# Fewer weight conversions in the first steps of attention, the 1e-9 added on GpSimd, and the scaled decay stored from another tile

## The chip, the cores and the metric

One core of a Trainium2 chip runs the whole program. The metric is the device time of one execution in microseconds (us), the median of three. The engines are TensorE (PE, its weight loads are PEld), VectorE (DVE), ScalarE (ACT), GpSimd (POOL) and SyncE (SP), whose queue issues nearly all DMA transfers. Each engine takes its instructions in the order in which they stand in the program, so an instruction that waits holds everything behind it on its engine.

## The reference

```python
# q, k, v: [4, 8, 576, 64], f: [4, 8, 576]
scores = scale * np.matmul(q, k.transpose(0, 1, 3, 2))
log_f = np.log(np.clip(f, 0.0001, 1.0))
cum = np.cumsum(log_f, axis=-1)
decay = cum[:, :, :, None] - cum[:, :, None, :]
scores = np.where(causal, -1000000000.0, scores + decay)
scores = scores - np.max(scores, axis=-1, keepdims=True)
attn = np.exp(scores)
attn = attn / (np.sum(attn, axis=-1, keepdims=True) + 1e-09)
x = np.matmul(attn, v)                    # then laid out as [2304, 512]
...
gate = 1.0 / (1.0 + np.exp(-(x @ w_gate)))     # w_gate, w_val: [512, 1536]
x = gate * (x @ w_val) @ w_out                 # w_out: [1536, 512]
...
h = x @ w_in                                   # [512, 2048]
out = (h * np.clip(h + 3.0, 0.0, 6.0) / 6.0) @ w_out2
```

## The kernel before

The weights arrive as float64 and are converted to pairs of float32 (a rounded part and the rest); the dense layers multiply such pairs with three matmuls each (`mm3`).

**Attention in steps.** The 16 pairs of heads are cut into four blocks of queries each; a block is a unit, and step t of the main loop (t = 0 to 66) starts unit t, so that pair p holds steps 4p to 4p + 3. Pairs 0 to 6 take their blocks upwards, the last block being the short one (64 queries of both heads together); pairs from 7 on (`KT`) take them downwards, load their queries and keys in another layout and transpose them on DVE. For a unit, PE computes scores into the banks `st` (`scores`); DVE adds the decay `dc` (`dt` for the short block, in which POOL has masked the future, `tail_decay`) and takes the least value in one pass (`least`, L500), into a tile `e` of the pool `ep`, which has seven buffers; ACT takes the exponential in place and sums it (L508); `norm` adds 1e-9 to the sums, takes the reciprocal on DVE (L543, L544) and has POOL scale `e` (L546). Step t runs `norm` for unit t - 1 and `flip` for unit t - 3: PE transposes `e` into `tt`, ACT copies that to `etA` and `etB`. At the last block of a pair, `values` multiplies with v, and `store` writes the result to DRAM, from where the first dense layer loads it again.

**Other work in the steps.** From step 4 on `conv.run` pays a rate into an account at each step; whenever it holds 1.0, one half (512 columns of 128 rows) of a weight tile is converted. A half is L107 and L108 on DVE, L111 on ACT, L114 on DVE, then the rounded part and the rest: both on POOL up to step 15 (L64, L65), on ACT (L62) and POOL (L65) from step 16. The halves come in the order `wg`, `wg`, `wv`, `wv`, `wg`, `wg`, `wv`, `wv`, four of `wo`, and four that are used only after attention. From step 23 on `fill.one()` puts one group of the first dense layer (12 matmuls of 512 columns: `pg`, `pv` or `po`) in each step, from step 30 on without those that hold `values`. A group whose weights' conversion has not been issued yet is not placed; the step then has no group, and all groups left are placed after attention.

**The scaled decay.** Pairs from 7 on need the decay times -8. `cumulate` makes the cumulative sum `cum` from the logarithms `fl`; after step 2 DVE writes the scaled copy to `eight`, a tile of the pool `ep`, and a DMA stores it in `cum_d[1]` (L1369, L1370). `fl` comes from the pool `ax` (two buffers, tag `x`), whose next use is the output tile `x` of `values`.

Of the kernel before, what the change touches and what calls it, by code (L numbers as in the profile page):

```python
# [7 lines left out]
F32 = mybir.dt.float32  # L8
# [4 lines left out]
ALU = mybir.AluOpType  # L13
# [7 lines left out]
def attn_moe_kernel(  # L21
# [13 lines left out]
    nc = tc.nc  # L35
    B, H, S, D = q.shape
# [3 lines left out]
    P = 128  # L40
    NP = H // 2
    NKT = 5
    NQ = 4
# [150 lines left out]
    conv = Converter()  # L194
# [43 lines left out]
    ep = att.enter_context(tc.tile_pool(name="ep", bufs=7))  # L238
# [50 lines left out]
    def cumulate():  # L289

        fl, one = (ax.tile([P, 2, S], F32, tag="x", name=nm)[: B * H] for nm in ("fl", "ones"))
        fl, ones, pick = fl[:, 0], one[:, 0], one[:, 1, : 2 * P].rearrange("p (j c) -> p j c", j=2)
        cum = ep.tile([P, S], F32, tag="e", name="cum")[: B * H]
        nc.scalar.dma_start(fl, f.rearrange("b h s -> (b h) s"))
        nc.vector.memset(ones, 1.0)
        nc.vector.tensor_scalar(fl, fl, 1.0e-4, 1.0, ALU.max, ALU.min)
        nc.scalar.activation(fl, fl, AF.Ln)
        nc.scalar.activation(one[:, 1, 2 * P : 2 * P + 1], fl[:, :1], AF.Exp)
        for j in range(2):
            nc.vector.tensor_scalar(pick[:, j], ones[:, :P], ident[: B * H, j : j + 1], 1.0, ALU.mult, ALU.mult)  # L300
        nc.vector.tensor_tensor_scan(cum, ones, fl, 0.0, ALU.mult, ALU.add)
        nc.sync.dma_start(cum_d[0], cum)
        return cum, pick

    def behind(i):
        return tc.issue_after(i.ins) if i is not None else ExitStack()
# [14 lines left out]
    class Pair:  # L321
# [217 lines left out]

        def norm(self, s):  # L540
            m, n = self.m[s], len(self.es[s])
            with behind(reads[-1]), tc.high_priority():
                nc.vector.tensor_scalar(m[:, 8 : 8 + n], m[:, 4 : 4 + n], 1.0e-9, None, ALU.add)  # L543
                pace["dve"] = nc.vector.reciprocal(m[:, 12 : 12 + n], m[:, 8 : 8 + n])  # L544
            for j, e in enumerate(self.es[s]):
                pace["pool"] = nc.gpsimd.tensor_scalar(e, e, m[:, 12 + j : 13 + j], 1.0, ALU.mult, ALU.mult)  # L546
# [504 lines left out]
    class Second:  # L1051
# [93 lines left out]
        def unit(self, k, x, ys, temps, between={}):  # L1145
            u1, u2, p5 = temps
            g, tt = self.ga[k % 2], nc.vector.tensor_tensor
            r11, r22, r12 = self.act(u1, g, 0, 0), self.act(p5, g, 1, 1), self.act(u2, g, 1, 0)
            r21 = self.act(x(), g, 0, 1)
            then = {1: (r11,), 2: (r11,), 3: (r11,), 4: (r22,), 5: (r12, r22, r22), 6: (r21, r12, r12, r21, r21)}  # L1150
            for s in range(7):
                if s in (1, 3):
                    y = ys.pop(0)()
                o = y if s % 2 else x()
                self.product(o, k, s, s in (0, 1, 3))
                if s in (0, 2, 3):
                    nc.scalar.copy({0: u1, 2: u2, 3: p5}[s], o)  # L1157
                elif s < 6:
                    c = {1: u1, 4: p5, 5: u2}[s]
                    tt(c, c, o, ALU.add)  # L1160
                for r in then.get(s, ()):
                    next(r)
                if k % NQ2 == NQ2 - 1:
                    self.load_block(k // NQ2 * 7 + 7 + s)
                if s in between:
                    between[s]()
# [59 lines left out]
    def warm_up(n):  # L1226
        if not warm:
            warm["z"] = a1.tile([P, 256], F32, tag="z", name="z").bitcast(BF16)
            with tc.high_priority():
                nc.vector.memset(warm["z"], 0.0)  # L1230
        z = warm["z"]
        for _ in range(n):
            o = psF.tile([P, 512], F32, tag="F", name="o")
            pe.matmul(o, z[:, :P], z, start=True, stop=True)
# [4 lines left out]
    EA = (nc.scalar, nc.gpsimd, nc.gpsimd)  # L1239
    EF = (nc.scalar, nc.scalar, nc.gpsimd)  # L1240
    WU = (8, 4, 4, 4)

    KD, KT, RT = 4, 7, 0

    CA, C0, CB, CC = 0.65, 4, (1.8, 1.0, 1.5, 1.7, 2.0), 1.0

    CE, CS = 0.38, 0.12


    NGA, NCA, GA = 2, 3, 1  # L1250

    NSA = 8
# [16 lines left out]
    units = [(p, s) for p in pairs for s in p.order]  # L1269
    pe.rows = True  # L1270
    warm_up(WU[0])
    cum, pick = cumulate()
    pairs[0].load()
    pairs[1].load()
    pairs[0].load_v()
# [88 lines left out]
    for t in range(len(units) + 3):  # L1364
        for job in (fixed, expo, norm, prep):
            job(t)
        if t == 2:
            eight = ep.tile([P, S], F32, tag="e", name="eight")[: B * H]
            nc.vector.tensor_scalar(eight, cum, -8.0, 1.0, ALU.mult, ALU.mult)  # L1369
            nc.sync.dma_start(cum_d[1], eight)  # L1370
        p, s = unit(t - 4)
        if p and s == p.order[-1] and p.hp == NP - 1 and p.b < NCA:
            done = p.b + 1
        p, s = unit(t - 5)
        if p and s == p.order[-1] and t < len(units) + 3:
            fill.load(p.b, p.hp + 1)
        if t >= C0:
            conv.run(CS if len(conv.jobs) <= 2 * NSA - 6 * NGA else CE if t < NQ * (KT - 1) else CA, EA if t < NQ * KD else EF)
        fill.n = done
    att.close()  # L1380
    pace["dve"] = None
# [63 lines left out]
```

## Time and profile before

| what | value |
|---|---|
| time, median of 3 (lowest, highest) | 1002.28 us (1002.18, 1002.36) |
| profiled execution, its own time | 1003.57 us |
| its span, first to last instruction | 1001.8 us |
| PE busy | 986.5 us (98%), 5733 matmuls |
| DVE, ACT, POOL busy | 530.9, 476.9, 290.5 us |
| mean granted TensorE clock | 0.998 |

Busy time is the union of an engine's instructions; a matmul's end is modelled, so a busy PE is not PE at its peak. The span leaves 1.77 us of the profiled execution outside, and the profiled execution is 1.29 us above the median.

### The profile page before, as it was taken

To read this page: it belongs to the slowest core of one execution; us is meant where nothing else is said; L and a number is where in the kernel's file an instruction comes from. 1 tells how busy PE (TensorE), PEld (TensorE's weight loads), DVE (VectorE), ACT (ScalarE), POOL (GpSimd) and SP (SyncE) were. 2 spreads that over 40 slices of the span, in tenths; PEclk is the share of its full clock that TensorE was granted. 3 is DMA by queue.
4 is the path that set the end of the run, shared out by engine and by line. 5 is a ranking of instruction groups with operands and counts; after the bars stand their busy time and mean duration, and the time that the engine had idled before them with its cause. 6 is when DMAs were issued, how large, how long until landed. Compare 5 with 4: busy or idle time off the path is not lost.

```text
span 1001.8 us, 16150 instructions
## 1 busy us (share of the span) xinstructions
PE 986.5 (98%) x5733; PEld 810.4 (81%) x5733; DVE 530.9 (53%) x1220; ACT 476.9 (48%) x1094; POOL 290.5 (29%) x360
## 2 busy tenths in 40 slices
PE   8889999999999999999999999999999999999998
PEld 4556766667688889988888888899899898998987
DVE  6777856645347543737777574553534443333322
ACT  6787677667634432424434343453444443433322
POOL 3675655545323220302334131111111111111110
PEclk9999999999999999999999999999999999999999
DMA  7999796744324352566977578654686845753211
GB/s 184 294 250 226 198 244 156 185 143 145 119 79 154 117 166 82 175 210 264 331 258 252 179 270 318 245 198 166 237 330 206 293 147 193 294 209 148 81 66 64
DMA packets 141072, 197.30 MB, mean 197 GB/s; under 512 B 84192, under 2 KB 93408, under 8 KB 136896
## 3 DMA queue, kind: packets, MB, share of 16 engines
q1 hardware_dynamic: 140944, 196.20, 59.9%
q8 instruction: 45, 0.74, 0.3%
q14 instruction: 35, 0.29, 0.1%
q10 hardware_dynamic: 48, 0.07, 0.0%
HBM read 142.88 MB, written 53.36 MB: 196 GB/s over the span
## 4 chain that ended last, share of the span: by engine, by line
PE 91%; DVE 3%; ACT 2%; DMA 2%; issue 1%; POOL 0%; SPq 0%; DVEq 0%; ACTq 0%; POOLq 0%
PE po L216 34%; PE pv L216 18%; PE u L216 17%; PE pg L216 15%; PE st L216 4%; PE tt L220 3%; DVE e L500 1%; DMA kn<-in_k_dram 1%; ACT e L508 1%; DMA cum_d<-eight 1%; DMA x_d<-x 0%; DVE raw L108 0%; ACT raw L111 0%; ACT etB L580 0%; PE o L216 0%
## 5 line engine op out<-in xcount | busy, mean ns | idle before, releaser
L216 PE MATMUL po<-w,big 128*128 128x512 f32 x864 | 200.5, 390 | 0.0
L216 PEld LDWEIGHTS po<-w,big 128*128 128x128 f32 x864 | 161.8, 188 | 32.8
L216 PE MATMUL pg<-big,wg 128*128 128x512 f32 (+1 forms) x720 | 161.9, 371 | 0.0
L216 PE MATMUL pv<-big,wv 128*128 128x512 f32 (+1 forms) x720 | 161.4, 371 | 0.0
L216 PE MATMUL po<-big,wo 128*128 128x512 f32 (+1 forms) x720 | 160.9, 371 | 0.2 <-DVE big L65 0.2
L216 PEld LDWEIGHTS pg<-big,wg 128*128 128x128 f32 x720 | 125.8, 189 | 27.2 <-issue 4.0
L216 PEld LDWEIGHTS pv<-big,wv 128*128 128x128 f32 x720 | 125.6, 189 | 26.8 <-issue 4.5
L216 PEld LDWEIGHTS po<-big,wo 128*128 128x128 f32 x720 | 125.6, 189 | 25.7 <-issue 2.2
L1160 DVE TENSOR_TENSOR h<-h,u 128x384 f32<-128x384 f32 x69 | 38.2, 554 | 154.0 <-PE u L216 154.0
L546 POOL TENSOR_SCALAR e<-e,m 128x256 f32<-128x256 f32 (+4 forms) x144 | 86.8, 617 | 48.8 <-DVE m L544 32.1
L508 ACT ACTIVATE e<-e,m 128x256 f32<-128x256 f32 (+4 forms) x144 | 83.6, 584 | 31.6 <-DVE m L500 20.3
L216 PE MATMUL u<-h,big 128*128 128x384 f32 x504 | 90.2, 336 | 0.4 <-DVE h L1160 0.4
L216 PE MATMUL u<-h,h 128*128 128x384 f32 x504 | 90.1, 336 | 0.0
L216 PEld LDWEIGHTS u<-h,big 128*128 128x128 f32 x504 | 88.3, 188 | 1.8 <-DVE h L1160 0.8
L216 PEld LDWEIGHTS u<-h,h 128*128 128x128 f32 x504 | 88.4, 188 | 1.0
L1109 POOL TENSOR_TENSOR big<-tail,big 128x384 fp32r<-128x384 f32 x30 | 30.5, 1018 | 196.5 <-PE u L216 115.5
L1157 ACT COPY h<-u 128x384 f32<-128x384 f32 x69 | 32.8, 475 | 111.5 <-PE u L216 111.5
L500 DVE CUSTOM_DVE_ANT_0 e<-st,dc 128x384 f32<-128x384 f32 (+3 forms) x110 | 53.5, 520 | 47.9 <-PE st L216 30.3
L872 DVE SCALAR_TENSOR_TENSOR sg<-sg,pv 128x512 f32<-128x512 f32 (+1 forms) x48 | 29.7, 618 | 92.3 <-PE pv L216 59.7
L111 ACT ACTIVATE raw<-raw 128x512 f32<-128x512 f32 x68 | 45.6, 682 | 67.1 <-DVE raw L108 64.5
L62 ACT CAST big<-sg 128x512 fp32r<-128x512 f32 (+1 forms) x60 | 34.8, 580 | 60.6 <-DVE sg L872 54.6
L114 DVE SCALAR_TENSOR_TENSOR raw<-raw 128x512 int32<-128x512 int32 x68 | 52.5, 782 | 19.4 <-ACT raw L111 18.9
(141 smaller groups left out, 1202.8 us busy)
## 6 DMA issues: line engine op xcount, KB each, us to landing
h<-xc_d SPq DMA_DIRECT2D x21, 768.0 KB, 7.2
big<-x_d SPq DMA_DIRECT2D x28, 512.0 KB, 5.8
raw<-in_moe_w_out_dram SPq DMA_DIRECT2D x28, 512.0 KB, 3.7
h<-wt_d SPq DMA_DIRECT2D x12, 1024.0 KB, 7.4
big<-wt_d SPq DMA_DIRECT2D x12, 1024.0 KB, 7.6
x_d<-x SPq DMA_DIRECT2D x16, 576.0 KB, 3.9
h<-wb_d SPq DMA_DIRECT2D x12, 768.0 KB, 4.6
big<-wb_d SPq DMA_DIRECT2D x12, 768.0 KB, 5.2
```

Of the source, the lines that this page charges most:

```text
L62: nc.scalar.copy(hi, src)
L111: nc.scalar.activation(e, e, AF.Copy, scale=2.0**-112)
L114: nc.vector.scalar_tensor_tensor(low, high, 3, low, ALU.logical_shift_left, ALU.bitwise_or)
L216: i = nc.tensor.matmul(*a, **k)
L220: i = nc.tensor.transpose(*a)
L500: i = nc.vector.tensor_tensor_reduce(out=e, in0=st, in1=d, op0=ALU.add, op1=ALU.min, scale=self.by, scalar=init, accum_out=m[:, a : a + 1],)
L508: nc.scalar.activation(e, e, AF.Exp, bias=m[:, a : a + 1], scale=-1.0, accum_out=m[:, 4 + b : 5 + b])
L546: pace["pool"] = nc.gpsimd.tensor_scalar(e, e, m[:, 12 + j : 13 + j], 1.0, ALU.mult, ALU.mult)
L872: pace["dve"] = nc.vector.scalar_tensor_tensor(sg, sg, 1.0, pv, ALU.add, ALU.mult)
L1109: (nc.vector if f else nc.gpsimd).tensor_tensor(lo, sg, hi.bitcast(F32), ALU.subtract)
L1157: nc.scalar.copy({0: u1, 2: u2, 3: p5}[s], o)
L1160: tt(c, c, o, ALU.add)
```

## The change

The account's rate is 0.24 instead of 0.38 in the first stretch, and that stretch ends at step 20 instead of 23; the rate of 0.65 behind it is the same. The 1e-9 is added on POOL, ahead of POOL's scaling of the same unit, and DVE's reciprocal waits for it. The scaled decay is written into `fl` instead of a tile of `ep`.

```diff
-        return cum, pick
+        return cum, pick, fl
...
     def norm(self, s):
         m, n = self.m[s], len(self.es[s])
+        with tc.high_priority():
+            nc.gpsimd.tensor_scalar(m[:, 8 : 8 + n], m[:, 4 : 4 + n], 1.0e-9, 1.0, ALU.add, ALU.mult)
         with behind(reads[-1]), tc.high_priority():
-            nc.vector.tensor_scalar(m[:, 8 : 8 + n], m[:, 4 : 4 + n], 1.0e-9, None, ALU.add)
             pace["dve"] = nc.vector.reciprocal(m[:, 12 : 12 + n], m[:, 8 : 8 + n])
...
-    CE, CS = 0.38, 0.12
+    CE, CS, CT = 0.24, 0.12, 21
...
-    cum, pick = cumulate()
+    cum, pick, eight = cumulate()
...
         if t == 2:
-            eight = ep.tile([P, S], F32, tag="e", name="eight")[: B * H]
             nc.vector.tensor_scalar(eight, cum, -8.0, 1.0, ALU.mult, ALU.mult)
             nc.sync.dma_start(cum_d[1], eight)
...
-            conv.run(CS if len(conv.jobs) <= 2 * NSA - 6 * NGA else CE if t < NQ * (KT - 1) else CA, EA if t < NQ * KD else EF)
+            conv.run(CS if len(conv.jobs) <= 2 * NSA - 6 * NGA else CE if t < CT else CA, EA if t < NQ * KD else EF)
```

On DVE, at the turn from step 6 to step 7 (the two L500 of 512 columns are unit 6, the one from `dt` is unit 7, L646 makes `x` for the finished pair), the kernel before has:

```order
L500 ISA e,m<-st,dc 128x512
L500 ISA m 128x1
L543 TENSOR_SCALAR m<-m 128x2
L544 RECIPROCAL m<-m 128x2
L107 TENSOR_SCALAR raw<-raw 128x512
L646 TENSOR_TENSOR x<-pv,x 128x256
L108 SCALAR_TENSOR_TENSOR raw<-raw 128x512
L114 SCALAR_TENSOR_TENSOR raw<-raw 128x512
L646 TENSOR_TENSOR x<-pv,x 128x320
L500 ISA e,m<-st,dt 128x288
```

The changed kernel has there (one line number higher):

```order
L500 ISA e,m<-st,dc 128x512
L500 ISA m 128x1
L545 RECIPROCAL m<-m 128x2
L647 TENSOR_TENSOR x<-pv,x 128x256
L647 TENSOR_TENSOR x<-pv,x 128x320
L500 ISA e,m<-st,dt 128x288
```

The first half's three DVE instructions have gone to step 8, and the add to POOL. On PE, at steps 32 to 35 (the first row is the transpose for unit 29, the next the scores of unit 32), the kernel before has:

```order
L220 MATMUL tt<-ident,e 128x64 x16
L216 MATMUL st<-kp,qz_144 128x288 x2
L216 MATMUL po<-big,wo_1692 128x512 x6
L216 MATMUL po<-big,wo_1883 128x512 x6
L220 MATMUL tt<-ident,e 128x64 x12
L216 MATMUL st<-kp,qp 128x512 x2
L216 MATMUL po<-big,wo_1692 128x512 x6
L216 MATMUL po<-big,wo_1883 128x512 x6
L220 MATMUL tt<-ident,e 128x64 x12
L216 MATMUL st<-kp,qp 128x384 x2
L216 MATMUL pv<-etB,vn_152 64x320 x6
```

The changed kernel has there:

```order
L220 MATMUL tt<-ident,e 128x64 x16
L216 MATMUL st<-kp,qz_144 128x288 x2
L220 MATMUL tt<-ident,e 128x64 x12
L216 MATMUL st<-kp,qp 128x512 x2
L220 MATMUL tt<-ident,e 128x64 x12
L216 MATMUL st<-kp,qp 128x384 x2
L216 MATMUL pv<-etB,vn_152 64x320 x6
```

Steps 32 and 33 hold no group any more; all later groups move by two places, and two stand behind attention that stood in it. On POOL, from unit 6's scaling to unit 8's (the 512-column L547 is unit 6, the 576-column one unit 7), the changed kernel has:

```order
L543 TENSOR_SCALAR m<-m 128x2
L547 TENSOR_SCALAR e<-e,m 128x512 x2
L386 AFFINE_SELECT dt<-dc 64x576 x2
L543 TENSOR_SCALAR m<-m 128x1
L547 TENSOR_SCALAR e<-e,m 128x576
L543 TENSOR_SCALAR m<-m 128x4
L547 TENSOR_SCALAR e<-e,m 128x128
```

Before, POOL had the same rows without the L543; now unit 7's add stands behind two masking passes for the next pair.

## Rows read from the trace of the kernel before

**Rows 1.** Stretch, length; busy PE, PEld, DVE, ACT, POOL; granted clock; DMA share, GB/s.

```profile
25.00:83.00 58.00, 50.21 (x500) 30.65 (x498) 45.40 (x163) 47.99 (x148) 41.78 (x60) 0.97 0.99 264
83.00:136.00 53.00, 52.13 (x380) 35.78 (x380) 39.30 (x118) 37.25 (x99) 31.10 (x41) 1.00 0.83 214
136.00:980.00 844.00, 843.56 (x4629) 716.96 (x4626) 423.78 (x865) 370.25 (x791) 206.13 (x233) 1.00 0.57 195
```

**Rows 2.** Timeline of DVE, steps 6 and 7: start, duration, [idle before <- releaser].

```profile
27.46 0.69 DVE L500 CUSTOM_DVE_ANT_0 e<-st,dc 128x512 f32<-128x512 f32 x1 [1.30 <-DMA cum_d<-eight]
...
28.36 0.41 DVE L107 TENSOR_SCALAR raw<-raw 128x512 int32<-128x512 int32 x1
...
31.50 0.45 DVE L500 CUSTOM_DVE_ANT_0 e<-st,dt 128x288 f32<-128x288 f32 x1
...
32.55 0.79 DVE L543 TENSOR_SCALAR m<-m 128x2 f32<-128x2 f32 x1
```

**Rows 3.** Timeline of PE, the scores of units 7 and 8.

```profile
28.61 1.24 PE L216 MATMUL st<-kp,qz 128*128 128x288 f32 x4
...
32.02 0.51 PE L216 MATMUL st<-masks,identb 128*128 128x384 bf16 x2 [2.06 <-DVE m L500]
```

**Rows 4.** Busy time by microsecond, one row of the stretch behind that wait.

```profile
33.00:34.00 1.00, 1.00 (x14) 1.00 (x12) 0.85 (x4) 1.00 (x4) 0.31 (x1) 0.50 1.20 191
```

**Rows 5.** Timeline of DVE, least values at steps 3, 11, 15, 19 and 23.

```profile
18.17 0.46 DVE L500 CUSTOM_DVE_ANT_0 e<-st,dt 128x288 f32<-128x288 f32 x1 [0.37 <-PE st L216]
...
43.94 0.46 DVE L500 CUSTOM_DVE_ANT_0 e<-st,dt 128x288 f32<-128x288 f32 x1 [0.31 <-PE st L216]
...
57.68 0.45 DVE L500 CUSTOM_DVE_ANT_0 e<-st,dt 128x288 f32<-128x288 f32 x1
...
69.73 0.45 DVE L500 CUSTOM_DVE_ANT_0 e<-st,dt 128x288 f32<-128x288 f32 x1
...
83.20 0.45 DVE L500 CUSTOM_DVE_ANT_0 e<-st,dt 128x288 f32<-128x288 f32 x1
```

**Rows 6.** One line's instructions, 20 to 136 us: ns least/median/most, first and last start.

```profile
L108 DVE SCALAR_TENSOR_TENSOR raw<-raw x12: 741/866/1123, 29.0 to 121.4; 128x512 int32<-128x512 int32 x12
...
L111 ACT ACTIVATE raw<-raw x12: 667/680/743, 29.8 to 122.3; 128x512 f32<-128x512 f32 x12
...
L114 DVE SCALAR_TENSOR_TENSOR raw<-raw x12: 683/694/993, 30.5 to 123.0; 128x512 int32<-128x512 int32 x12
```

**Rows 7.** Timelines of POOL and DVE: a half's rest; unit 15's masking and reciprocal.

```profile
32.02 1.30 POOL L65 TENSOR_TENSOR wg<-raw,wg 128x512 fp32r<-128x512 f32 x1
...
61.58 1.40 POOL L386 TENSOR_SCALAR_AFFINE_SELECT dt<-dc 64x576 f32<-64x576 f32 x2
...
61.87 0.15 DVE L544 RECIPROCAL m<-m 128x1 f32<-128x1 f32 x1
```

**Rows 8.** Groups of 25 to 83 us: busy us, mean ns | idle before.

```profile
L546 POOL TENSOR_SCALAR e<-e,m 128x128 f32<-128x128 f32 x10 | 3.7, 373 | 3.3 <-ACT e L508 1.3 <-DVE m L544 1.2 <-PE tt L220 0.7
L543 DVE TENSOR_SCALAR m<-m 128x2 f32<-128x2 f32 x9 | 3.0, 335 | 0.0
```

**Rows 9.** Timeline of PE, steps 32 to 34.

```profile
125.17 1.24 PE L216 MATMUL st<-kp,qz 128*128 128x288 f32 x4
126.03 2.80 PE L216 MATMUL po<-big,wo 128*128 128x512 f32 x10
...
131.17 3.06 PE L216 MATMUL po<-big,wo 128*128 128x512 f32 x12
...
135.37 1.03 PE L216 MATMUL pv<-etB,vn 128*64 128x320 f32 x6
```

**Rows 10.** Timeline of DVE, the least values of units 32 and 33.

```profile
127.55 0.45 DVE L500 CUSTOM_DVE_ANT_0 e<-st,dt 128x288 f32<-128x288 f32 x1
...
131.37 0.69 DVE L500 CUSTOM_DVE_ANT_0 e<-st,dc 128x512 f32<-128x512 f32 x1 [1.23 <-POOL e L546]
```

**Rows 11.** Timeline of SP's queue, the store of the scaled decay.

```profile
21.49 0.51 SPq L1370 DMA_DIRECT2D cum_d<-eight  x1
```

## Prediction

> **What bounds the kernel now.** I read the busy time by stretch first. From 136 to 980 us PE is busy 843.56 of 844 us: nothing there waits, and no edit here changes PE's work, so time can be won or lost only ahead of it. From 25 to 83 us, the steps before the first group of the dense layer, PE is busy 50.21 of 58 us, with a mean granted clock of 0.97, while ACT is busy 48 and DVE 45; from 83 to 136 us it is busy 52.13 of 53 [rows 1]. So 7.8 us of idle PE and, by the clock (0.03 of 58), up to 1.7 us of slow PE lie in the first stretch, and 0.9 us in the second. The timelines of DVE and PE then show one place in detail: unit 6's least value waits 1.30 us for the DMA from `eight`, whose buffer it takes over; behind it stand the first half's instructions, L107 at 28.36, and unit 7's least value comes only at 31.50 [rows 2], 2.9 us after its scores began at 28.61; PE, which needs that bank, waits 2.06 us [rows 3]. Behind this wait the granted clock is 0.50, the lower of its two levels, 1.2 GHz [rows 4].
>
> **When the halves come.** The account gives the steps. Before: 0.38 from step 4 passes whole numbers at steps 6, 9, 11, 14, 17, 19 and 22, then with 0.65 at 24, 26, 27, 29 and 30. After: 0.24 passes at 8, 12, 16 and 20, then 0.65 at 22, 23, 25, 27, 28, 30, 31 and 33. Up to step 22 there are five halves in place of seven. The last `wo` half is issued at step 33 in place of 30, so steps 32 and 33 have no `po` to place, as the order on PE shows.
>
> **The first stretch: gain.** Take as a measure the least value of the short block, once in four steps. It starts at 18.17, 31.50, 43.94, 57.68, 69.73 and 83.20 [rows 2, 5]; the pitches are 13.3, 12.4, 13.7, 12.1 and 13.5 us, with 1, 1, 2, 1 and 2 halves. After they hold 0, 1, 1, 1 and 2.
> - Steps 3 to 7: both the wait for `eight` and the half go. Unit 7's scores start at 28.61 because PE still multiplies with v until then, so DVE can begin on its first bank half-way through these scores (1.24 us, [rows 3]), at about 29.3 in place of 31.50: -2.2 us.
> - Steps 7 to 11: one half as before, but PE does not fall to the lower level. Of the 1.7 us above I take 0.9, because part of that work lay beside DVE's: -0.9 us, bounds 0 and 1.7.
> - Steps 11 to 15: one half in place of two. Two halves cost 13.5 and 13.7, one 12.1: -1.6 us.
> - Steps 15 to 23: the same number of halves; nothing.
>
> A half has 0.41 + 0.87 + 0.69 = 2.0 us on DVE and 0.68 on ACT [rows 2, 6], so 1.6 per half fits. Together -4.7 us.
>
> **The add on POOL.** DVE loses one small instruction in every step; the nine of 128x2 in this stretch take 0.335 us in the mean, one of them 0.79 [rows 2, 8], ending at 33.34 just as POOL's subtraction ends at 32.02 + 1.30 = 33.32 [rows 7]. What that frees on DVE I count as nothing by itself, since the pitches are set by ACT and PE as much (48 and 50 of 58 us). The price: the reciprocal now waits for POOL, and behind it on DVE stand the next least values, for which PE waits. POOL works in order, and unit 4p + 3's add stands behind two maskings. At unit 15 these run from 61.58 to 62.98, while the reciprocal ran at 61.87 [rows 7]: there it would come at least 1.1 us later, less what POOL itself gains because the reciprocal ahead of it comes earlier (the add ahead of it, up to 0.79, is gone). POOL's add is not in the trace: its nearest row is the 128x128 scaling, 0.37 us [rows 8], the other bound is DVE's own 0.15; I take 0.2. In two of five pairs I expect 0.2 to 0.3 us on the path: +0.5 us, bounds 0 and 3.5 (0.7 in each of five).
>
> **The store from `fl`.** It is issued some 9 us earlier, ahead of the third pair's loads; SP spends 0.51 us on it [rows 11], hidden because these loads are needed only at step 4. DVE's scaling moves from step 2 to the scan, where DVE next waits for PE's transposes: nothing. The buffer of `fl` is next written by `values` at step 6, some 10 us after. Were these covers gone, 0.5 us each.
>
> **Steps 32 to 35: loss.** The two groups taken out begin at 126.03 and 131.17; a group's row is 3.06 us, and the next matmul starts a little before its end, so I take 2.95 each, 5.9 us. From unit 32's scores at 125.17 to the multiplication with v at 135.37 PE takes 10.2 us [rows 9]; some 4.3 us of it is attention. But DVE is late there: unit 32's least value starts at 127.55, 1.5 us after its scores, and unit 33's at 131.37, of which 1.23 is a wait for PE [rows 10]. After, DVE has one half less behind it at step 29 (-1.4 us, the half with what it delays) and one more in front of unit 32 (+2.0): 128.1. From there to unit 33's least value it had 3.8 - 1.2 = 2.6 us of work, less the two adds and transposes now ahead: about 130.2. Its first half ends at 130.9, POOL's scaling of unit 31 at about 131.4 (four of 0.37 behind a reciprocal at 129.6), then about 1.1 us of transposes and scores: v begins at 132.5. That is 2.9 us earlier, where 5.9 us of groups went behind attention: a loss of 3.0. With 0.7 us at step 35, where the first `po` group finds its last half hardly finished (a half takes 0.41 + 0.87 + 0.68 + 0.69 and 1.30 on POOL even if nothing waits, [rows 2, 6, 7], and step 33's starts only behind unit 33's least value), and 0.3 for a possible fall of the clock in two waits of 2 us: +4.0 us, bounds 1.5 (DVE and ACT catch up during the groups before) and 7.0 (all 5.9 lost, and the clock). The two groups behind attention cost what they cost before, counted here already.
>
> **Sum.** -4.7 + 0.5 + 4.0 = -0.2, and -0.4 for the waits between 83 and 136 us of which some go with DVE's adds (0.9 us in all): -0.6 us. The profiled span of 1001.8 would be 1001.2, its execution 1003.0; on the median, 1.29 lower, 1001.7 us.
>
> **The rivals.** 0.2% (2.0 us) is about what a measurement of this kernel can tell from no change.
> - *The lost groups cost little.* If DVE reaches unit 32 early, the two short steps run at 2 us each and only 1.5 us is lost: -4.7 + 0.5 + 1.5 - 0.4 = -3.1, 999.2 us. For it: DVE had 39.3 of 53 us of work and loses its adds [rows 1]. Against: it is late by 1.5 us at just this place [rows 10]. 0.32.
> - *POOL's queue sets the pace.* If in each of five pairs unit 4p + 3's add comes 0.7 us after DVE wants it, the first stretch gives back 3.5 in place of 0.5: 1004.7 us, slower. It decides once the maskings end more than 0.5 us after the reciprocal's place in most pairs; at unit 15 they end 1.1 later [rows 7]. Against: DVE's least value behind it waited for PE there anyway. The Trainium skill, in "GPSIMD Engine Reference", section 4.1 Engine selection, wants elementwise work on a tile on VectorE, not on GpSimd. No row has the two engines on the same small tile. 0.14.
> - *The loss is at its upper bound*: 7.0 us, 1004.7. For it: two waits of 2 us, like the one behind which the clock fell [rows 3, 4]. 0.08.
> - *The wait for `eight` is only replaced*, by another reader of the same buffer: then 1.3 us less is won, 1003.0, the same by measure. The buffer that comes up instead is unit 2's, whose transposes stood two steps earlier, so this is within the case that I forecast.
>
> **How the numbers follow.** Gain and loss nearly cancel: 0.46 for within 0.2% (1000.3 to 1004.3), at 1001.7, its own range 1000.3 to 1003.9. Faster by more than 0.2% is the first rival, 0.32; slower by more the second and third, 0.22. The range goes to both: 998.6 (gain 5.2, loss 1.5) to 1004.7, with about a tenth left out on either side.
>
> **What would show it.** Unit 6's least value has no wait for a DMA, and 31 to 36 us run at the higher clock; the short block's pitch to step 7 is about 11 us, that from step 11 to 15 about 12; the first `pg` group starts near 78.8 (83.0 now, less 4.2), the multiplication with v of step 34 near 128 (135.4, less 4.2, 0.4 and 2.9). PE idles 3 to 4 us between the scores of units 32 and 35. Wrong would be the prediction if PE waits there for under 2 us, if DVE waits for POOL's adds over 1 us in the first stretch, or if the groups after attention bring idle time to PE.

## The result, and the profile after

The changed kernel takes 1010.08 us (median of 6 runs, 1008.18 to 1011.47), the kernel before in the same runs 1002.32 (1001.17 to 1005.44): ratio 1.0072, 95% interval 1.0054 to 1.009. It is slower; the prediction was 1001.7, and its range ended at 1004.7. The profiled execution took 1010.16 us with a span of 1008.4, 6.6 us more than the span of before; PE is busy 989.6 us, DVE 518.2, ACT 477.9 and POOL 302.0, and the mean granted clock is 0.994.

The three stretches of [rows 1] in the changed kernel (length; busy PE, PEld, DVE, ACT, POOL; granted clock; DMA share, GB/s):

```profile
25.00:83.00 58.00, 51.16 (x510) 31.12 (x506) 42.88 (x152) 49.25 (x152) 40.50 (x74) 1.00 0.91 243
83.00:136.00 53.00, 47.81 (x343) 31.80 (x345) 36.56 (x103) 36.20 (x96) 36.55 (x53) 0.91 0.87 230
136.00:980.00 844.00, 843.56 (x4618) 715.53 (x4615) 415.31 (x830) 368.95 (x789) 212.13 (x263) 1.00 0.56 195
```

The first stretch is better: PE is busy for 51.16 us in place of 50.21, always at the higher clock. The second is worse: 47.81 in place of 52.13, at a mean clock of 0.91. In the third PE is as busy as before.

DVE's least values of the short blocks, the measure of [rows 2, 5]:

```profile
18.57 0.46 DVE L500 CUSTOM_DVE_ANT_0 e<-st,dt 128x288 f32<-128x288 f32 x1 [0.57 <-PE st L216]
...
29.75 0.46 DVE L500 CUSTOM_DVE_ANT_0 e<-st,dt 128x288 f32<-128x288 f32 x1 [0.21 <-PE st L216]
...
41.65 0.46 DVE L500 CUSTOM_DVE_ANT_0 e<-st,dt 128x288 f32<-128x288 f32 x1 [0.21 <-PE st L216]
...
54.15 0.46 DVE L500 CUSTOM_DVE_ANT_0 e<-st,dt 128x288 f32<-128x288 f32 x1 [0.21 <-PE st L216]
...
66.65 0.46 DVE L500 CUSTOM_DVE_ANT_0 e<-st,dt 128x288 f32<-128x288 f32 x1 [0.21 <-PE st L216]
...
80.22 0.44 DVE L500 CUSTOM_DVE_ANT_0 e<-st,dt 128x288 f32<-128x288 f32 x1
```

The pitches are 11.2, 11.9, 12.5, 12.5 and 13.6 us, and the wait for the store of `eight` is gone. PE's timeline behind them, from the first group on, and from unit 32 on (it answers to [rows 9]):

```profile
79.47 2.31 PE L216 MATMUL pg<-big,wg 128*128 128x512 f32 x9
84.15 0.96 PE L216 MATMUL pg<-big,wg 128*128 128x512 f32 x3 [2.37 <-DMA big<-x_d]
...
87.56 3.63 PE L216 MATMUL pg<-big,wg 128*128 128x512 f32 x12
...
125.18 1.24 PE L216 MATMUL st<-kp,qz 128*128 128x288 f32 x4
128.64 0.58 PE L220 MATMUL tt<-ident,e 64*128 64x64 f32 x12 [2.22 <-ACT etB L581]
129.04 1.27 PE L216 MATMUL st<-kp,qp 64*128 64x512 f32 x4
131.24 0.37 PE L220 MATMUL tt<-ident,e 64*128 64x64 f32 x2 [0.93 <-ACT etB L581]
132.42 1.28 PE L220 MATMUL tt<-ident,e 64*128 64x64 f32 x10 [0.81 <-POOL e L547]
133.48 1.60 PE L216 MATMUL st<-kp,qp 64*128 64x384 f32 x4
135.01 3.07 PE L216 MATMUL pv<-etB,vn 128*64 128x320 f32 x20
...
139.83 3.01 PE L216 MATMUL po<-big,wo 128*128 128x512 f32 x12
...
143.42 1.24 PE L216 MATMUL st<-kp,qz 128*128 128x288 f32 x4
```

The first `pg` group starts at 79.47, where before it started at 82.98. But inside it PE waits 2.37 us for a load of x, and unit 32's scores come at 125.18, where they stood before (125.17). Then PE waits three times, 3.96 us together, in the two steps that have no group. The granted clock in one microsecond behind either place (columns as above):

```profile
86.00:87.00 1.00, 1.00 (x12) 0.91 (x10) 0.66 (x1) 0.97 (x3) 0.00 (x0) 0.50 1.00 344
131.00:132.00 1.00, 0.37 (x2) 0.21 (x2) 0.66 (x4) 0.95 (x4) 1.00 (x2) 0.50 1.25 239
```

0.50 is the lower level, 1.2 GHz; by the rows of single microseconds it lasts from about 85.5 to 88.9 and from 129.8 to 136.7 us.

**An account of the span.** The short blocks' scores (units 23, 27, 32 and 36) cut every program of this study at the same places. From unit 27 to unit 32 all nineteen take 21.6 to 21.7 us, and from unit 36 to the end 858.8 to 860.0 us with every group in its place, or 864.3 to 865.0 with two groups left over. So a profile's span differs, but for 0.1 us, only by the last four columns of this table (us; the first column is the difference of the medians, for e15 that of one run):

| run | time, to before | unit 23 | 23 to 27 | 32 to 36 | 36 to end |
|---|---|---|---|---|---|
| before | | 81.87 | 21.68 | 17.81 | 858.8 |
| changed | +7.8 | 78.36 | 25.20 | 18.24 | 865.0 |
| e1 halves | +9.9 | 79.55 | 23.69 | 20.59 | 864.3 |
| e2 add | +2.8 | 79.62 | 23.32 | 17.63 | 859.2 |
| e3 fl | +0.1 | 79.73 | 22.45 | 17.78 | 858.9 |
| e4 ct19 | +6.6 | 78.39 | 25.72 | 21.98 | 859.4 |
| e5 gap | +8.2 | 77.85 | 27.29 | 17.94 | 864.6 |
| e6 ct17 | +7.8 | 79.62 | 30.69 | 17.65 | 860.0 |
| e7 fl, ct17 | +5.6 | 81.67 | 27.03 | 17.80 | 859.5 |
| e8 x on ACT | +11.3 | 85.53 | 20.78 | 19.32 | 864.9 |
| e9 before, lite | +11.1 | 93.74 | 20.82 | 17.12 | 858.8 |
| e10 halves, lite | +13.1 | 85.59 | 29.51 | 13.56 | 864.6 |
| e11 add, not 128x1 | +3.2 | 79.94 | 22.48 | 18.06 | 859.4 |
| e12 fl, one half | -0.2 | 79.90 | 22.62 | 17.77 | 858.9 |
| e13 e12 and add | +5.2 | 78.78 | 28.72 | 17.65 | 859.4 |
| e14 halves, fl | +9.4 | 80.86 | 24.95 | 19.93 | 864.5 |
| e15 add again | +2.5 | 79.58 | 25.53 | 17.64 | 859.2 |
| e16 x early | +4.8 | 77.76 | 21.78 | 19.44 | 865.0 |
| e17 e13, x early | +4.7 | 78.83 | 28.73 | 17.63 | 859.2 |

For the changed kernel: -3.5 in the front, +3.5 from unit 23 to 27, +0.4 from 32 to 36, +6.2 behind, +6.6 in all. One trace is one execution (the kernel before has spans from 999.2 to 1004.1 in its other runs), so a difference under about 1.5 us is read from the medians alone. The profiled execution of the kernel before was a long one, 1.25 us above the median of its runs, that of the changed kernel 0.08: this is why the columns add up to 6.6 and the medians to 7.8. Nor is the fall of the clock at 33 us [rows 4] usual: with it the mean clock is 0.998, and in 53 of the 71 runs of the kernel before beside the experiments it is 0.999 or 1.000, with a median span of 1000.4. So part of what the fronts in the table gain on 81.87 is owed to that one execution.

### The profile page after: what moved, and what is told of

Same layout as the page of the kernel before. It is cut to its first block, busy times and chain, and to the rows that moved or that the text cites. A ratio compares the mean times of both kernels' runs of the same rounds, so it can differ in the third digit from the quotient of the medians.

```text
span 1008.4 us, 16126 instructions
## 1 busy us (share of the span) xinstructions
PE 989.6 (98%) x5733; PEld 812.0 (81%) x5733; DVE 518.2 (51%) x1156; ACT 477.9 (47%) x1096; POOL 302.0 (30%) x422
## 4 chain that ended last, share of the span: by engine, by line
PE 93%; DVE 2%; POOL 2%; DMA 1%; issue 1%; ACT 0%; SPq 0%; POOLq 0%; DVEq 0%; ACTq 0%
PE po L216 34%; PE pv L216 18%; PE u L216 17%; PE pg L216 14%; PE st L216 5%; PE tt L220 3%; POOL e L547 1%; POOL dt L386 1%; PE o L216 1%; DMA x_d<-x 1%; DVE e L500 0%; DMA big<-x_d 0%; DVE raw L108 0%; DMA kn<-in_k_dram 0%; DVE xp L891 0%
## 5 line engine op out<-in xcount | busy, mean ns | idle before, releaser
L547 POOL TENSOR_SCALAR e<-e,m 128x256 f32<-128x256 f32 (+4 forms) x144 | 87.2, 618 | 35.5 <-DVE m L545 23.7
L111 ACT ACTIVATE raw<-raw 128x512 f32<-128x512 f32 x68 | 45.5, 681 | 64.3 <-DVE raw L108 61.8
L500 DVE CUSTOM_DVE_ANT_0 e<-st,dc 128x384 f32<-128x384 f32 (+3 forms) x110 | 53.3, 519 | 42.1 <-PE st L216 41.3
```

Source lines behind the costliest of these rows:

```text
L111: nc.scalar.activation(e, e, AF.Copy, scale=2.0**-112)
L500: i = nc.vector.tensor_tensor_reduce(out=e, in0=st, in1=d, op0=ALU.add, op1=ALU.min, scale=self.by, scalar=init, accum_out=m[:, a : a + 1],)
```

## The experiments

**First set: the parts.** Theory A, formed from the traces: the two steps without a group are the loss, and the gain of the front is lost to the late load of x. B puts the loss on the add, C on the store from `fl`, which would bring a new order into SP's queue.

Run e1_halves:

```diff
-    CE, CS = 0.38, 0.12
+    CE, CS, CT = 0.24, 0.12, 21
...
-            conv.run(CS if len(conv.jobs) <= 2 * NSA - 6 * NGA else CE if t < NQ * (KT - 1) else CA, EA if t < NQ * KD else EF)
+            conv.run(CS if len(conv.jobs) <= 2 * NSA - 6 * NGA else CE if t < CT else CA, EA if t < NQ * KD else EF)
```

> Only the constants of the conversions are changed (0.24 a step and the limit of 21 steps); the 1e-9 stays on DVE and the scaled sums go through an exponentials' tile as before. PE gets its groups in the order of the changed kernel: none between the scores of units 30 and 33. Theory A (the two steps without a group are the loss, with the clock that falls in them, and the front stretch's gain is lost to the late load of x): 1007 to 1010 us, at least 5 us above the kernel before in the same runs; the po of step 35 at 139.4 to 140.5 us as in the changed kernel, granted clock 0.50 somewhere in 128 to 137 us. Theory B (the add on GpSimd is the loss): within 2 us of the kernel before. Theory C (the store from the logarithms' tile reorders SP's queue, and that is the loss): also within 2 us of the kernel before.

Measured: 1012.22 us, ratio 1.009 (1.0062 to 1.0117). That is above A's range; B and C, as they stand, fall as the main cause. Alone, the late halves cost 2 us more in the median than the whole change, though the two intervals overlap. The two steps without a group are 32 and 33 here too.

Run e2_add:

```diff
+            with tc.high_priority():
+                nc.gpsimd.tensor_scalar(m[:, 8 : 8 + n], m[:, 4 : 4 + n], 1.0e-9, 1.0, ALU.add, ALU.mult)
             with behind(reads[-1]), tc.high_priority():
-                nc.vector.tensor_scalar(m[:, 8 : 8 + n], m[:, 4 : 4 + n], 1.0e-9, None, ALU.add)
```

> Only the 1e-9 is added on GpSimd, everything else as before; PE's groups stand as before. Theory A: 1002 to 1004 us, no more than 1.5 us above the kernel before, since each of the small adds takes 0.2 to 0.5 us on an engine that is busy for 30% of the span. Theory B: 1006 us or more, with the reciprocal's waits for POOL as PE's last releaser in many steps. Theory C: as theory A.

Measured: 1005.12 us, ratio 1.0021 (1.001 to 1.0032). Between the two expectations: the add has a price, 2.8 us, without being the loss.

Run e3_fl:

```diff
-        return cum, pick
+        return cum, pick, fl
...
-    cum, pick = cumulate()
+    cum, pick, eight = cumulate()
...
-            eight = ep.tile([P, S], F32, tag="e", name="eight")[: B * H]
```

> Only the scaled sums are written into the logarithms' tile and stored from it; conversions and add as before. Theory A: 1000.5 to 1003 us: the wait of 1.3 us in step 6 of the kernel before is gone, but the pitch of steps 7 to 15 stays near 13 us, since it is set by the halves of conversion, and the first pg starts 0 to 2 us earlier than 82.98. Theory B: the same. Theory C: 1006 us or more, and PE waits for the load of x in its first group.

Measured: 1002.44 us, ratio 1.0002 (0.9989 to 1.0014). The front is 2.1 us shorter, a little more than expected; 0.8 of that is lost between units 23 and 27 in its trace, and nothing shows in the median (its trace is set against the long execution of the kernel before).

Run e4_ct19, all 12 halves issued by step 31:

```diff
-    CE, CS, CT = 0.24, 0.12, 21
+    CE, CS, CT = 0.24, 0.12, 19
```

> The changed kernel with one number more: the rate of 0.24 holds for 19 steps in place of 21, so that all 12 halves are issued by step 31, and PE has its groups in every step, in the order of the kernel before. The add is on GpSimd and the store from the logarithms' tile, as in the changed kernel. Theory A: 998.5 to 1003 us, about 6 to 9 us below the changed kernel; the front stretch as in the changed kernel (first pg near 79.5 us), PE's wait of about 2.4 us for the load of x in that group still there, and po in units 31 and 32 without the clock at 0.50. Theory B or C: 1007 us or more, since add and store are as in the changed kernel.

Measured: 1008.93 us, ratio 1.0066 (1.0041 to 1.0091). A's number is missed; it is what B and C gave, which e1_halves, e2_add and e3_fl rule out as the main cause. PE has its groups in the order of before, and waits inside the first `po` group for the last half of its weights:

```profile
126.59 2.43 PE L216 MATMUL po<-big,wo 128*128 128x512 f32 x9
130.09 0.50 PE L216 MATMUL po<-big,wo 128*128 128x512 f32 x1 [1.07 <-ACT wo L62]
130.95 0.49 PE L216 MATMUL po<-big,wo 128*128 128x512 f32 x1 [0.35 <-DVE big L65]
132.44 0.50 PE L216 MATMUL po<-big,wo 128*128 128x512 f32 x1 [1.00 <-POOL wo L65]
```

32 to 36 takes 21.98 us, 4.2 more than before: the half that is late costs there with the group as it did without. The wait for x is only 0.16 us here, but 4.0 us go between units 23 and 27 all the same.

**Second set: late halves, or the gap.** Theory D: the halves are only too late, and if they end as before nothing is lost. Theory E: two halves fewer in the front cost in themselves, since the work falls where there is no room for it.

Run e5_gap takes e4_ct19 and leaves out the groups of steps 32 and 33:

```diff
-        if t > NQ * (NP + 1) + 2 and not (last and p.i != NP + 1 and t < len(units)):
+        if t > NQ * (NP + 1) + 2 and t not in (32, 33) and not (last and p.i != NP + 1 and t < len(units)):
             fill.one()
```

> The kernel of run e4_ct19 (0.24 for 19 steps, halves done by step 31, 1008.9 us), with PE's group left out at steps 32 and 33 and given later, so that PE's groups come in exactly the order of the changed kernel while the conversions of steps 32 to 35 are gone. In e4_ct19 PE waited 2.4 us inside its first po group for the last half of conversion. Theory A (two steps without a group cost what the groups would have filled): 1008 to 1011 us, no better than e4_ct19 and near the changed kernel's 1010; PE idle 3 us or more between the scores of units 32 and 34, clock 0.50 behind it. Theory D (what costs is the late conversion work, on which PE waits either way): 1003 to 1006 us, since the last half is done before a group asks for it, and PE waits under 1.5 us at steps 32 to 35.

Measured: 1011.07 us, ratio 1.0091 (1.0073 to 1.0108), at the upper end of A's range. It did not tell as cleanly as meant: the half of step 31 still ran at 125 to 133 us, so "the conversions gone" was not reached. ACT's scaling of that half (L111) waited 1.84 us for DVE's L108, with the copy to `etB` behind it, and PE waited 2.18 us for that copy, as in the changed kernel.

Run e6_ct17 sets `CT` to 17 (the 12th half at step 30, as before); run e7_fl_ct17 has the add on DVE besides.

> The changed kernel with the rate of 0.24 held for 17 steps in place of 21: the 12th half is issued at step 30 as in the kernel before, PE's groups in the order of before, add on GpSimd, store from the logarithms' tile. Theory D (late halves are the loss, the add is 1 to 3 us of its own as run e2_add had it): 1002 to 1006 us; no wait of PE over 0.5 us for wo in its first po group; the first pg near 79.5 us as in the changed kernel. Theory E (fewer halves in the front stretch cost in themselves, whenever they end, since DVE, ACT and GpSimd have to make them up between units 16 and 31 and hold PE there): 1006 to 1009 us, with waits of PE of 3 us or more in 85 to 125 us.

> As run e6_ct17 but with the 1e-9 added on DVE as before. If the add's cost of 2.8 us, as run e2_add has it, holds here too: 1 to 3 us below e6_ct17. Theory D: 999.5 to 1003 us, no slower than the kernel before. Theory E: 1004 us or more. If the add costs only where it stands in front of late halves: within 0.5 us of e6_ct17.

Measured: 1010.7 us (1.0077, 1.0062 to 1.0092) and 1008.52 (1.0055, 1.0039 to 1.0071). D falls: 32 to 36 is as before in both, no group is lost, and 23 to 27 is 9.0 and 5.4 us longer. E has the place right (its number for e6_ct17, at most 1009, is too low), but its reason, no room on the engines, is not shown. In e7_fl_ct17, PE's longest wait there is for POOL's scaling (mean clock 0.89 from 92 to 122 us), and POOL had itself waited for the load of the decay:

```profile
93.45 1.36 PE L220 MATMUL tt<-ident,e 64*128 64x64 f32 x16 [2.72 <-POOL e L546]
```

```profile
90.62 0.41 POOL L449 TENSOR_SCALAR_AFFINE_SELECT dz<-dc 128x256 f32<-128x256 f32 x1 [6.16 <-DMA dc<-cum_d]
```

In e6_ct17 PE's longest is 3.01 us for DVE's `x` (L647), which stood behind a half that waited for its weights to be loaded:

```profile
82.46 0.43 DVE L107 TENSOR_SCALAR raw<-raw 128x512 int32<-128x512 int32 x1 [2.90 <-DMA raw<-in_moe_w_val_dram]
```

So engines stood idle for loads in this stretch; what the halves' work alone costs there was not separated from it.

Run e8_after_actx:

```diff
-        nc.sync.dma_start(
+        (nc.scalar if c == 0 and kc == KC - 1 else nc.sync).dma_start(
```

> The changed kernel with one edit: the fourth piece of x is loaded by ScalarE's queue, where it does not stand behind the six loads of queries and keys (4.89 and 2.71 us of issue) in SP's queue. If the 2.37 us that PE waits for it in the first pg group, and the clock of 0.50 behind it, take the front stretch's gain away: the wait falls under 0.5 us, no clock under 0.9 in 80 to 92 us, the scores of unit 32 come 2 to 3.5 us earlier than 125.18, and the time is 1006 to 1008 us. If another engine sets that stretch's pace: the wait moves on to GpSimd's or DVE's work before 125 us, the scores of unit 32 come within 1 us of 125.18, and the time is within 1 us of the changed kernel's 1010.1.

Measured: 1014.23 us, ratio 1.0125 (1.0106 to 1.0144). A new wait took the place of the old one. ACT, which takes its instructions in order, stood 6.44 us for the store of x ahead of the load, and PE stood 5.36 us up to 78.40 (the profile names no releaser for it; by the times it is the copy to `etB` behind that store):

```profile
77.23 1.07 ACT L581 COPY etB<-tt 128x512 f32<-128x512 f32 x2 [6.44 <-DMA x_d<-x]
```

So it doesn't tell what the wait for x is worth. With that wait moved into the front, 23 to 27 takes 20.78 us, less than before.

**Third set: the work itself, and how much of it.** Runs e9_before_lite and e10_halves_lite leave the bit work out of the conversions in the steps of attention:

```diff
         low, high = raw[:, :, 0], raw[:, :, 1]
+        if pace["lite"]:
+            return high.bitcast(F32).rearrange("p (a b) -> p a b", a=a_)
```

> The kernel before with conversions of weights that leave out their bit work in the attention's loop: the three integer operations of DVE and the scaling of ScalarE (L107, L108, L111, L114) are not done, the two halves of a weight are written from the high words as they are; PE's instructions and their order are those of the kernel before. It gives the price of that work where the kernel before has it. If conversions set the pace only in the front stretch: 985 to 997 us, the pitch from unit 3 to unit 7 near 11 us and all of the gain before 83 us.

> Run e1_halves (only the constants changed, 1012.2 us) with the same bit work left out as in e9_before_lite; PE's instructions and their order are those of e1_halves, with no group at steps 31 and 32. Theory A (the two steps without a group cost what the groups would have filled, conversions or not): 4 to 7 us above e9_before_lite, PE idle or at clock 0.50 for 3 us or more in the stretch of units 32 to 34. Theory E (what costs is the conversion work itself, which falls where DVE, ScalarE and GpSimd have no room for it): within 2 us of e9_before_lite.

Measured: 1013.59 us (1.0109, 1.0096 to 1.0122) and 1015.62 (1.0121, 1.0106 to 1.0135). With less work both are slower than the kernel before, which no theory had. Without DVE's operations in front of it, POOL's part of a half moves ahead of the scaling that PE waits for. In e9_before_lite PE waits five times, 9.9 us together, for that scaling ahead of unit 23, each time behind POOL's L64 or L65; the mean clock is 0.88 from 25 to 80 us, and DVE is busy for only 26.4 of these 55 us. The first of the five places, where POOL waits for the weights besides:

```profile
25.97 0.64 POOL L64 TENSOR_SCALAR wg<-raw 128x512 fp32r<-128x512 f32 x1 [2.45 <-DMA raw<-in_moe_w_gate_dram]
26.58 0.74 POOL L548 TENSOR_SCALAR e<-e,m 128x576 f32<-128x576 f32 x1
27.29 1.29 POOL L65 TENSOR_TENSOR wg<-raw,wg 128x512 fp32r<-128x512 f32 x1
28.57 1.62 POOL L548 TENSOR_SCALAR e<-e,m 128x128 f32<-128x128 f32 x4
```

As a price of the work the pair is inconclusive. One column still speaks: in e10_halves_lite 32 to 36 takes 13.56 us with no group in two steps; before, with two groups more (5.9 us), it takes 17.81, so attention and the group of step 35 had 11.9. Without the bit work the gap costs 1.7 us there; in e1_halves, with it, 20.59 - 11.9 = 8.7. By this estimate most of the price of these steps is the conversion work that has come to stand in them, with the clock that falls behind it, and not the missing groups.

Run e11_add_not1 is e2_add with the add on DVE where n is 1:

> Run e2_add (only the 1e-9 on GpSimd, 1005.1 us) with one change: where a unit has a single tile of exponentials (128x1 sums), the add is on DVE as before. In e2_add the reciprocal behind that 128x1 add waited 3.83 us, since the add stood on GpSimd behind a conversion, two scalings and the masking of the decay, and PE lost 2.0 us at 93 to 96 us after it. If that queue is the add's price: 1002 to 1004 us and no wait of DVE for GpSimd's add over 1 us. If the price lies in the other adds (their 0.2 to 0.5 us on GpSimd in each of the front's units): 1004.5 to 1006 us.

Measured: 1005.75 us, ratio 1.0025 (1.0017 to 1.0034). The wait of the reciprocal behind the 128x1 add is gone, and the price is not: that add alone does not explain it.

Run e12_fl_31 is e3_fl with `CE, CT = 0.31, 20`:

> Run e3_fl (only the store from the logarithms' tile, 1002.4 us) with the rate of conversions at 0.31 for 20 steps in place of 0.38 for 24: one half later at step 20 than e3_fl, one half earlier than the changed kernel, the last half issued at step 31, and PE's groups as before. Theory E: each half that is postponed from the front costs more behind unit 16 than it gives back, so 1003.5 to 1007 us, between e3_fl and e7_fl_ct17 (1008.5). If one half later were free, with only the second half too late: 1000 to 1003 us.

Measured: 1002.39 us, ratio 1.0001 (0.9993 to 1.001). E missed this one: one half later, placed like this, is free; two, as e7_fl_ct17 places them, are not.

**Fourth set: what was open.** Run e13_add_fl_31 is the changed kernel with `CE, CT = 0.31, 20`; run e14_halves_fl is the changed kernel with the add on DVE; run e15_add_again is e2_add for a second profile.

> The changed kernel with the conversions one half later in place of two (0.31 for 20 steps): run e12_fl_31 (1002.4 us) with the 1e-9 on GpSimd. If the add's price of 2.8 us in run e2_add is its own: 1004 to 1006.5 us. If the changed kernel's loss is the second late half alone and the add costs only beside the old rate: 1001.5 to 1003.5 us. If the add is what makes a late half dear: 1007 us or more.

> The changed kernel with the 1e-9 added on DVE as before: the two late halves and the store from the logarithms' tile. If the parts add up (halves alone 1012.2, add 2.8 above before, the store nothing): 1006.5 to 1009 us, 1 to 3.5 below the changed kernel. If the add gives back something beside the late halves, since it frees DVE: 1010 to 1013 us. PE waits again 2 us or more between the scores of units 32 and 34, with the clock at 0.50, in either case.

> Run e2_add once more for another profile of it: the profiled execution of e2_add was its fastest (span 1001.4, clock 0.999), while eight of its ten had a mean clock of 0.997 or 0.998 and spans of 1002.5 to 1004.6. If the add's price is a fall of the clock that it makes more frequent: a stretch at clock 0.50 to 0.9 ahead of 140 us, behind an idle of PE of 2 us or more that ends with GpSimd or with DVE work that waited for GpSimd. If the price is plain waiting: no such stretch, and 2 us more of idle PE than in e2_add.

Measured: 1008.02 us (1.0054, 1.004 to 1.0068), 1012.26 (1.0096, 1.0081 to 1.0111) and one run of 1005.36. The parts do not add up: the add costs 5.4 us beside one late half (5.2 for e13 and -0.2 for e12) and gives back about 2 beside two (the changed kernel to e14, where the intervals overlap). The second profile of the add has the clock at 1.00 from the start to 980 us, so in this execution its price is plain waiting; eight of the ten runs of e2_add have a mean clock of 0.997 or 0.998, and what a fall of the clock costs in those no trace shows. POOL's and DVE's timelines of e15_add_again:

```profile
87.91 0.41 POOL L449 TENSOR_SCALAR_AFFINE_SELECT dz<-dc 128x256 f32<-128x256 f32 x1 [7.67 <-DMA dc<-cum_d]
88.28 1.29 POOL L65 TENSOR_TENSOR wv<-raw,wv 128x512 fp32r<-128x512 f32 x1
89.55 1.36 POOL L547 TENSOR_SCALAR e<-e,m 128x512 f32<-128x512 f32 x2
90.86 1.39 POOL L386 TENSOR_SCALAR_AFFINE_SELECT dt<-dc 64x576 f32<-64x576 f32 x2
92.35 0.20 POOL L543 TENSOR_SCALAR m<-m 128x1 f32<-128x1 f32 x1
```

```profile
92.58 0.17 DVE L545 RECIPROCAL m<-m 128x1 f32<-128x1 f32 x1 [6.09 <-POOL m L543]
```

POOL waits for the load of the decay; the scaling behind it comes late (PE waits 1.94 us for it), and so does the add, for which DVE's reciprocal waits 6.09 us and, behind it, PE another 1.08 and 0.99. In e2_add the load came in time and only the last two waits are there: its span is 2.2 us shorter.

Runs e16_xrow and e17_xrow_31 take the wait for x away from the changed kernel and from e13_add_fl_31, by reading the last piece of x from rows that are stored a pair earlier:

```diff
         t0, T = chunks[c]
+        kc -= c == 0 and kc == KC - 1
         x = xr[ring["x"] % len(xr)][:, :, :T]
```

> The changed kernel with one address changed: the fourth piece of x for the first chunk is read from the rows of the third, which are in memory a pair earlier, so SP issues that load some 14 us sooner and nothing waits for the store of the fourth pair; the result is computed from the wrong rows there, and everything else stands as in the changed kernel. If the wait of 2.37 us for that load and the clock of 0.50 behind it are where the front stretch's 3.5 us went: no wait there, no clock under 0.9 in 80 to 92 us, the scores of unit 32 at 122 to 123.5 us and the time 1006.5 to 1008.5 us. If DVE and GpSimd hold PE there as in run e4_ct19, where that wait was only 0.16 us: waits of 2.5 us or more for them in 85 to 125 us, and the time 1009 to 1011 us.

> Run e13_add_fl_31 (1008.0 us, where PE waited 4.45 us for that piece of x and the clock was 0.86 in 80 to 92 us) with the same address changed. If that wait is what the add on GpSimd costs there: 1003 to 1005 us. If the wait moves on to GpSimd's or DVE's work: 1006.5 to 1009 us.

Measured: 1006.8 us (1.0047, 1.0032 to 1.0062) and 1006.71 (1.0042, 1.0028 to 1.0056). In e16_xrow the front's gain is kept to unit 32, whose scores start 4.0 us earlier than in the changed kernel, and about 3 us of it reach the time; the two steps without a group then cost more (19.44 us from unit 32 to 36), again behind `etB`, and with the clock at 0.50 from about 124.7 to 135.0 us:

```profile
121.16 1.24 PE L217 MATMUL st<-kp,qz 128*128 128x288 f32 x4
124.63 0.86 PE L221 MATMUL tt<-ident,e 64*128 64x64 f32 x12 [2.23 <-ACT etB L582]
...
128.41 1.28 PE L221 MATMUL tt<-ident,e 64*128 64x64 f32 x10 [0.82 <-POOL e L548]
```

In e17_xrow_31 the wait of 4.45 us for x is replaced by one of 3.99 us for POOL's scaling, ahead of which POOL had waited 8.56 us for the load of the decay; at most 1.3 us are won.

## Why the prediction was wrong, point by point

**The front: right, a little too large.** The wait for `eight` went, the clock stayed at the higher level from 25 to 80 us, and the first `pg` group came at 79.47 (foretold: 78.8). The gain is 3.5 us where 4.2 (4.7 less 0.5) was foretold. By the pitches, steps 3 to 7 gave 2.1 (2.2 foretold), 7 to 11 0.5 (0.9), 11 to 15 1.2 (1.6), and 15 to 23, put at nothing, gave back 0.5. Part of the gain belongs to the one execution that was profiled: a fall of the clock as long as the one counted as 0.9 us is not in most runs of the kernel before, and the sum took off 1.29 us for that execution besides. Whether the add frees DVE in the front, put at nothing, is open: e2_add is 2.2 us earlier at unit 23, but set against the same execution.

**From 83 to 136 us: the step that failed first.** The sum carried the front's gain to the end and took 0.4 us more off this stretch. From unit 23 to 27 it measured +3.5: the stretch ran at its pace only because PE came late. The prediction took PE's 52.13 of 53 us for a stretch in which nothing but 0.9 us of waits could change, and did not look at when the loads land. SP's queue, changed kernel, then before:

```profile
71.85 4.89 SPq L352 DMA_DIRECT2D qn<-in_q_dram  x4
76.83 2.71 SPq L352 DMA_DIRECT2D kn<-in_k_dram  x2
79.64 0.45 SPq L205 DMA_DIRECT2D big<-x_d  x1
```

```profile
76.93 0.99 SPq L205 DMA_DIRECT2D big<-x_d  x1
...
82.28 0.38 SPq L365 DMA_DIRECT2D dc<-cum_d  x1
```

The load of x is issued 2.7 us later than before, now behind two loads of keys, and lands 4.5 us after its issue, at 84.1; PE, which before reached that place after 85 us, is there at 81.8. The new place in the queue came with the halves and not with the store, as C had it: in e1_halves and e12_fl_31 the load is issued at 79.85 and 79.75, behind two loads of keys, in e3_fl at 74.94, ahead of them. e16_xrow shows that this wait, with the clock behind it, is what took the gain in the changed kernel: without it 23 to 27 takes 21.78 us (its load of the decay is also issued 1.8 us earlier, which was not separated). It is not the only one that would: with a wait for x of at most 0.16 us, e4_ct19, e7_fl_ct17 and e17_xrow_31 lose 4 to 7 us between units 23 and 27 to waits for POOL, DVE and ACT and, in the last two, to the lower clock; ahead of that POOL had waited 5.00, 6.16 and 8.56 us for a DMA.

**Steps 32 to 35: the mechanism was right, the term too small.** Foretold were 4.0 us, bounds 1.5 and 7.0; it is 6.6 (0.4 and the two groups' 6.2). The chain was right up to DVE: unit 32's least value was foretold for 128.1 and came at 128.31, unit 33's for 130.2 and came at 130.35. (The wait of 1.23 us in [rows 10], which the prediction gives to PE, is put down to POOL's scaling in its row.) The idle of PE there, foretold as 3 to 4 us, is 3.96. The step that failed is "POOL's scaling of unit 31 at about 131.4", with v at 132.5. POOL's timeline in the changed kernel:

```profile
130.00 0.65 POOL L547 TENSOR_SCALAR e<-e,m 128x128 f32<-128x128 f32 x1 [1.56 <-DMA kn<-in_k_dram]
130.62 1.29 POOL L65 TENSOR_TENSOR wo<-raw,wo 128x512 fp32r<-128x512 f32 x1
131.90 1.27 POOL L547 TENSOR_SCALAR e<-e,m 128x256 f32<-128x256 f32 x3
```

The rest of a half (L65, 1.29 us) stands in the middle of that scaling, which ends at 133.2. ACT has the same ahead of PE's transposes, in the wait of 2.22 us:

```profile
126.87 0.68 ACT L111 ACTIVATE raw<-raw 128x512 f32<-128x512 f32 x1 [1.82 <-DVE raw L108]
127.45 1.05 ACT L581 COPY etB<-tt 128x512 f32<-128x512 f32 x2
```

And the clock, put at 0.3 us, was at the lower level for 6.8 us: the scores at 133.48 take 1.60 us where 0.86 is usual, and the multiplication with v behind them 3.07 where before it took 2.27, 1.5 us together. v begins at 135.01, 0.4 us earlier after unit 32's scores than before where 2.9 was foretold. The 0.7 us at step 35 came out by luck: from v to unit 36's scores it is 0.8 us more, but that is v at the lower clock; the `po` group there takes 3.01 us at 139.83 and waits for no half.

**The add on POOL.** Put at 0.5 us, bounds 0 and 3.5; alone it costs 2.8 (1.0 to 3.2 by the interval). The place was wrong: in the front DVE waits for POOL's adds 2.0 us in six waits, none over 0.54, and the front gets shorter all the same: the sign of being wrong that the prediction named, over 1 us there, came without the loss. In the two profiles of the add alone the price falls at steps 25 and 26, in e15_add_again behind the load of the decay. The Trainium skill, in "GPSIMD Engine Reference", section 4.1 Engine selection, wants elementwise work on VectorE; in the median the runs agree (e2 to before, e13 to e12). The rows of e15_add_again put it down to the queue: the add itself takes 0.20 us there and 0.19 to 0.51 in the changed kernel. Why e11_add_not1 keeps the price is open, and so is the sign beside two late halves.

**The store from `fl`.** Nothing, as foretold (e3_fl).

**The rivals.** The nearest was the loss at its upper bound, 7.0 us with the clock, 1004.7; that loss came (6.6), but the rival still counted on the front's gain. That POOL's queue sets the pace happens, at another place. That this gain could be lost to a load was no rival at all. Of the 8.4 us missed, 3.9 lie there (+3.5 for -0.4), 2.6 in steps 32 to 35, 0.7 in the front, and 1.2 in the step from the profile to the median: the sum took 1.29 off, and the changed kernel's profile is only 0.08 above its median.

## What to carry to other kernels

Work that is put off is due later: before moving it, read what runs beside it at its new place, on every in-order engine that it passes, and not their busy shares. When an engine is made earlier, list the loads it will meet and when they land; a gain ends at the first that does not come earlier too. An instruction moved to an idle engine waits for everything ahead of it there, an operation that waits for a DMA above all.

## What the runs showed that I had not expected

Taking work off DVE made the program 11 us slower (e9_before_lite): as far as its trace tells, what DVE did had also kept POOL's part behind the scaling that PE waits for. With the add on DVE, one half later costs nothing, two cost 5.6 to 9.9 us. And no version tried is faster than the kernel before: the best, e12_fl_31 and e3_fl, are the same by measure.
